# Routing logits added up by products with a matrix of ones and zeros, and fewer count products, in an attention and mixture-of-experts kernel

## Chip, cores and metric

The kernel runs on one core of a Trainium2 chip. The metric is the device time of one execution in microseconds, the median of several executions.

## What is computed

The reference runs attention with a sigmoid in place of the softmax over 8 batches of 12 heads, 448 tokens and a head size of 64. Its output, 3584 tokens of 768 numbers, goes into a layer of 8 experts, where each token is sent to the expert of its largest logit:

```
scores = scale * q @ k.T - log(S);  attn = sigmoid(scores);  x = attn @ v
logits = x @ w_gate                       # 3584 x 8
e_idx  = argmax(logits)
gate_w = softmax(logits)[e_idx]
eom    = sigmoid(x @ w_output_gate)[e_idx]
out[token] = gate_w * eom * (relu(x @ w1[e_idx]) @ w2[e_idx])
```

## The kernel before

**Attention.** TensorE works through 168 units: `scores` (L626) makes four products 64x64 by 64x448 in fp32 for two heads, ScalarE applies the sigmoid (L634), and `values` (L636) multiplies by v two units later. Seven units make a group of two head pairs; there are 24 groups, three to a batch. VectorE adds halves and transposes each finished head pair (L644 to L655), and SyncE loads the next group and stores x to DRAM.

**Gates.** After every second group, `gates(k)` (L668) multiplies four head pairs by the gate weights, both kinds of gates at once (L671). The array is cut into four column strips of 32; strip e holds head pair e's share of 16 logits for 448 tokens, and 16 rows of zeros. VectorE copies or adds these 128x448 partial sums to SBUF tile `gl` (L676 to L683).

**Routing.** `route(b)` (L229) turns a batch's `gl` into positions in the experts' lists. It is a generator, and `attention` calls its steps at fixed places of the unit loop (the named steps in L710 and L701), so the order of work on every engine is written out by hand:

- "logits": TensorE transposes `gl` in four chunks of 112 tokens (L238) into PSUM bank `mm_ps`. VectorE adds the four strips (L239), and in five short operations finds the largest logit and a 0/1 matrix `oh`, 112 tokens by 4 chunks by 8 experts, in bf16 (L242 to L246).
- "counts": TensorE counts tokens with bf16 products. A strict triangle `tri` times `oh` gives each token's rank within its chunk (L254); products of all ones add the counts of earlier chunks (L256, three products), and four more make the batch's totals `cnt` (L260).
- "places": ScalarE copies ranks and totals out of PSUM (L262); GpSimd works out positions and weights. "rows" scatters four lists of rows to DRAM.

Seven batches go through these steps inside the attention units. The last batch's run inside the first expert slot, where `side()` (L769) calls them between the `layer1` products (L467, L468).

**Start.** `constants()` (L129) issues the identity matrix, `wg`, the ones, the triangle and small tables, nearly all on GpSimd. `attention` then clears a `warm` tile on VectorE (L691), loads three groups, and issues 20 products on `warm` (L695) ahead of the first scores.

**Experts.** Each slot takes 256 tokens of one expert. Weights are split into high and low parts by ScalarE and VectorE, and TensorE does the products in fp32r (L467, L468, L490 to L492; half slots L574 to L576).

Of the kernel before, what the change touches and what calls it, by code (L numbers as in the profile page):

```python
# [9 lines left out]
F32 = mybir.dt.float32  # L10
F32R = mybir.dt.float32r
BF16 = mybir.dt.bfloat16
I32 = mybir.dt.int32
AF = mybir.ActivationFunctionType
ALU = mybir.AluOpType
AX = mybir.AxisListType
# [4 lines left out]
B, H, S, D = 8, 12, 448, 64  # L21
NPAIR = H // 2
E = 8
# [3 lines left out]
CP = 112  # L27
NCH = S // CP
# [23 lines left out]
class Kernel:  # L52
# [76 lines left out]
    def constants(self):  # L129
        nc = self.nc  # L130
        cp = self.const = self.pool("const")
        dram = self.pool("dram", space=DRAM)
        self.x_dram = dram.tile([NT * 4, Q4], F32, name="x_dram")
        self.lst = dram.tile([E * CAP + TS, 6], F32, name="lst")

        self.bias_s = cp.tile([128, 1], F32, name="bias_s")
        nc.vector.memset(self.bias_s, -math.log(S))
        nc.scalar.activation(self.warm_t(cp), self.bias_s, AF.Sigmoid)
        self.ident = cp.tile([128, 128], F32, name="ident")
        make_identity(nc, self.ident)  # L140
        self.wg = cp.tile([128, NPAIR, 32], F32, name="wg")
        nc.gpsimd.memset(self.wg, 0.0)
        nc.gpsimd.dma_start(self.wg[:, :, 0:16], self.wgo)
        self.ones = cp.tile([CP, 128], BF16, name="ones")
        nc.gpsimd.memset(self.ones, 1.0)
        self.tri = cp.tile([CP, 128], BF16, name="tri")
        nc.gpsimd.memset(self.tri, 1.0)
        nc.gpsimd.affine_select(self.tri, self.tri, pattern=[[1, 128]], compare_op=ALU.is_gt, fill=0.0,
                                base=0, channel_multiplier=-1)
        iota = lambda t, pattern, base=0: nc.gpsimd.iota(  # L150
            t, pattern=pattern, base=base, channel_multiplier=0, allow_small_or_imprecise_dtypes=True)
        self.rev = cp.tile([CP, NCH, E], F32, name="rev")
        iota(self.rev, [[0, NCH], [-1, E]], E)
        self.run = cp.tile([128, E], F32, name="run")
        nc.gpsimd.memset(self.run, 0.0)
        self.off = cp.tile([128, E], F32, name="off")
        self.ebase = cp.tile([128, E], F32, name="ebase")
        iota(self.ebase, [[CAP, E]])
        self.ids = cp.tile([1, E], F32, name="ids")
        iota(self.ids, [[1, E]])  # L160
        self.kts = cp.tile([1, 2, 16], F32, name="kts")
        iota(self.kts, [[HS, 2], [TS, 16]])
        self.meta = cp.tile([CP, B, NCH, 6], F32, name="meta")
        self.tok = cp.tile([CP, 2, NCH], I32, name="tok")
        self.tokf = cp.tile([CP, NCH, 4], F32, name="tokf")
        self.step = cp.tile([CP, B, 4], F32, name="step")
        nc.gpsimd.iota(self.tok[:, 0], pattern=[[CP, NCH]], base=0, channel_multiplier=1)
        iota(self.step, [[S, 4 * B]])
        nc.gpsimd.iota(self.meta[:, :, :, 4], pattern=[[S, B], [CP, NCH]], base=0, channel_multiplier=1,
                       allow_small_or_imprecise_dtypes=True)  # L170
        self.lt32 = [cp.tile([32, 6, 32], F32, name="lt32")]
        self.eps = cp.tile([CP, NCH], F32, name="eps")
        nc.gpsimd.memset(self.eps, 1e-9)
        self.one8 = cp.tile([1, E], F32, name="one8")
        nc.gpsimd.memset(self.one8, 1.0)
        self.last_e = cp.tile([1, 1], F32, name="last_e")
        self.taken = cp.tile([1, E], F32, name="taken")
        slots = EARLY + LATE_N
        self.lts = cp.tile([128, slots, 2, 2], I32, name="lts")
        self.ltb = cp.tile([128, E, 1, 2], I32, name="ltb")  # L180
        self.lxs = cp.tile([128, slots, 8], I32, name="lxs")
        self.lxb = cp.tile([128, E, 4], I32, name="lxb")
        self.slots = cp.tile([1, 2, LATE_N], F32, name="slots")
        for i, st in enumerate((1, TS)):
            iota(self.slots[:, i], [[st, LATE_N]])
        gl = [cp.tile([128, n], F32, name=f"gl{i}") for i, n in enumerate((2 * TS, S))]
        self.gl = [g[:, 0:S] for g in gl]
        self.sums = [gl[0][:, 0:TS], gl[0][:, TS:2 * TS], gl[1][:, 0:TS]]
        self.route_tiles()

    def row_words(self):
        v, tok = self.nc.vector, self.tok
        v.tensor_scalar(tok[:, 1], tok[:, 0], 5, None, ALU.logical_shift_right)
        v.tensor_scalar(tok[:, 0], tok[:, 0], 31, None, ALU.bitwise_and)
        v.tensor_scalar(tok[:, 0], tok[:, 0], S // 32, None, ALU.mult)
        v.tensor_tensor(tok[:, 0], tok[:, 0], tok[:, 1], ALU.add)
        v.tensor_copy(self.tokf, tok[:, 0].unsqueeze(2).broadcast_to([CP, NCH, 4]))
        for b in range(B):
            v.tensor_tensor(self.meta[:, b, :, 0:4], self.tokf,
                            self.step[:, b].unsqueeze(1).broadcast_to([CP, NCH, 4]), ALU.add)  # L200
# [11 lines left out]
    def route_tiles(self):  # L212
        rp = self.pool("route")
        t = lambda n, shape, dt=F32: rp.tile(shape, dt, name=n)
        self.R = dict(
            lg=t("lg", [CP, NCH, 16]),
            mx=t("mx", [CP, NCH]), fi=t("fi", [CP, NCH]), df=t("df", [CP, NCH, E]), rk=t("rk", [CP, NCH, E]),
            oh=t("oh", [CP, NCH, E], BF16), sg=t("sg", [CP, 3, NCH, E]),
            pc=t("pc", [128, (NCH + 1) * E]), pos=t("pos", [CP, NCH, E]), posf=t("posf", [CP, NCH]),
            t4=t("t4", [CP, NCH, 4]), t2=t("t2", [CP, NCH, 2]),  # L220
            posi=t("posi", [CP, NCH], I32), den=t("den", [CP, NCH]), eom=t("eom", [CP, NCH]))
# [7 lines left out]
    def route(self, b):  # L229
        nc, R = self.nc, self.R  # L230
        g, v = nc.gpsimd, nc.vector
        tt = g.tensor_tensor
        bc = lambda t: t.unsqueeze(2).broadcast_to([CP, NCH, E])
        tt(self.off, self.run, self.ebase, ALU.add)
        yield "logits"
        ps = self.mm_ps
        for c in range(NCH):
            nc.tensor.transpose(ps[0:CP, 128 * c:128 * c + 128], self.gl[b % 2][:, c * CP:(c + 1) * CP], self.ident)  # L238
        v.tensor_reduce(R["lg"], ps[0:CP, 0:128 * NCH].rearrange("p (c e x) -> p c x e", c=NCH, e=4)[:, :, 0:16, :],  # L239
                        AX.X, ALU.add)  # L240
        lg = R["lg"][:, :, 0:E]
        v.tensor_reduce(R["mx"], lg, AX.X, ALU.max)  # L242
        v.tensor_tensor(R["df"], lg, bc(R["mx"]), ALU.subtract)
        v.scalar_tensor_tensor(R["rk"], R["df"], 0.0, self.rev, ALU.is_ge, ALU.mult)
        v.tensor_reduce(R["fi"], R["rk"], AX.X, ALU.max)
        v.tensor_tensor(R["oh"], R["rk"], bc(R["fi"]), ALU.is_equal)  # L246
        yield "counts"
        sg, oh = R["sg"], R["oh"]
        nc.scalar.activation(sg[:, 0], R["df"], AF.Sigmoid)
        nc.scalar.activation(sg[:, 1], R["df"], AF.Sigmoid, scale=-1.0)  # L250
        nc.scalar.activation(sg[:, 2], R["lg"][:, :, E:16], AF.Sigmoid)
        ps = self.mm_ps
        pre, cnt = ps[:, 0:NCH * E], ps[:, NCH * E:(NCH + 1) * E]
        nc.tensor.matmul(pre, self.tri, oh.rearrange("p c e -> p (c e)"), start=True, stop=False)  # L254
        for c in range(NCH - 1):
            nc.tensor.matmul(pre[:, (c + 1) * E:].rearrange("p (c e) -> p c e", e=E), self.ones,  # L256
                             oh[:, c:c + 1, :].broadcast_to([CP, NCH - 1 - c, E]),
                             start=False, stop=(c == NCH - 2))
        for c in range(NCH):
            nc.tensor.matmul(cnt, self.ones, oh[:, c, :], start=(c == 0), stop=(c == NCH - 1))  # L260
        yield "places"
        nc.scalar.copy(R["pc"], ps[:, 0:(NCH + 1) * E])  # L262
        v.reciprocal(sg[:, 1], sg[:, 1])
# [487 lines left out]
    def build(self, phases="abc"):  # L751
        tc, nc = self.tc, self.nc
        ms = tc.manual_schedule()
        ms.__enter__()
        self.constants()
        self.memory()
        with tc.tile_pool(name="attn", bufs=1) as p, tc.tile_pool(name="rows", bufs=1) as q:
            rt = self.attention(p, q)
        self.late_memory()
# [110 lines left out]
```

## Time and profile before

| | |
|---|---|
| Median of 3 runs | 802.03 us (799.63, 802.03, 804.19) |
| Profiled execution, its own time | 802.2 us |
| Its span, first to last instruction | 800.4 us |
| TensorE busy (matmul) | 784.6 us, 98% |
| TensorE weight loads | 582.3 us, 73% |
| VectorE, ScalarE, GpSimd busy | 498.4, 494.9 and 338.4 us |
| Mean granted TensorE clock | 0.996 |

The span is what the trace covers; the time is some 2 us longer. PE stands for matrix products and PEld for the weight loads that run beside them. A product's row begins when it can be issued and includes its way through the array, so rows overlap: how much a group of products holds TensorE up is read from start to start, not from durations. Attention lasts to about 285 us, the experts from there to the end.

### The profile page before, as it was taken

How to read it: one execution, taken by the hardware profiler on the slowest of the kernel's cores; microseconds unless marked ns; L12 is line 12 of the kernel's file. 1: busy time of each engine (PE TensorE's matmuls, PEld its weight loads, DVE VectorE, ACT ScalarE, POOL GpSimd, SP SyncE). 2: the span in 40 equal slices, each digit the busy share in tenths (PEclk: the TensorE clock that was granted, in tenths of full speed). 3: DMA queues.
4: the chain of work that ended last, by engine and by line, in shares of the span. 5: the costliest groups of instructions: out<-in, count | busy, mean ns of one | idle time of the engine just before them, and what ended most of it. 6: DMA issues, size and time to landing. Idle time of an engine off the chain costs nothing. (4 is left out here: it accounts for less than half of the span.)

```text
span 800.4 us, 15091 instructions
## 1 busy us (share of the span) xinstructions
PE 784.6 (98%) x5772; PEld 582.3 (73%) x5772; DVE 498.4 (62%) x731; ACT 494.9 (62%) x665; POOL 338.4 (42%) x454
## 2 busy tenths in 40 slices
PE   9999999999999899899999999999999999999996
PEld 4333433333333379799999999999999999999885
DVE  2344435444455667877785657766667767667687
ACT  5666666666668556556665556655666557565685
POOL 4003302310333456647646265543646725445344
PEclk9999999999999999999999999999999999999999
DMA  6353553525448420237228471182274211749382
GB/s 255 131 209 128 158 200 139 193 85 208 170 173 347 154 90 21 77 123 266 75 75 290 166 270 51 49 312 79 61 259 156 64 45 41 267 131 336 110 314 59
DMA packets 32311, 126.80 MB, mean 158 GB/s; under 512 B 5536, under 2 KB 7824, under 8 KB 28257
## 3 DMA queue, kind: packets, MB, share of 16 engines
q1 hardware_dynamic: 22288, 100.81, 35.5%
q0 software_dynamic: 9936, 24.88, 9.4%
q8 instruction: 50, 0.82, 0.4%
q14 instruction: 37, 0.29, 0.1%
HBM read 153.15 MB, written 23.64 MB: 221 GB/s over the span
## 5 line engine op out<-in xcount | busy, mean ns | idle before, releaser
L467 PE MATMUL ps<-rounded 128*128 128x512 f32 x672 | 234.8, 393 | 2.0 <-DVE gl L476 2.0
L634 ACT ACTIVATE a<-ps,bias_s 128x896 f32<-128x896 f32 x168 | 169.2, 1008 | 102.5 <-PE ps L632 96.1
L468 PE MATMUL ps<-rounded 128*128 128x256 f32 x672 | 188.1, 280 | 0.0
L404 POOL DMA_INDIRECT plain<-x_dram,lxs x120 | 170.2, 1418 | 38.3 <-issue 37.0
L490 PE MATMUL ps<-w2h,h 128*128 128x384 f32 x480 | 160.6, 335 | 0.0
L492 PE MATMUL ps<-w2h,h 128*128 128x384 f32 x480 | 160.4, 334 | 0.0
L491 PE MATMUL ps<-w2l,h 128*128 128x384 f32 x480 | 160.4, 334 | 0.0
L632 PE MATMUL ps<-kqv 64*64 64x448 f32 x1344 | 158.6, 543 | 0.5 <-ACT a L634 0.4
L641 PE MATMUL ps<-a,kqv 64*64 64x448 f32 x1344 | 156.7, 538 | 0.0
L427 DVE TENSOR_TENSOR w2l<-plain,w2h 128x1536 fp32r<-128x1536 f32 x60 | 105.3, 1758 | 78.3 <-ACT w2h L426 68.1
L467 PEld LDWEIGHTS ps<-rounded 128*128 128x128 f32 x672 | 125.7, 187 | 31.3 <-DVE gl L476 2.7
L504 POOL DMA_INDIRECT out<-y,lts x28 | 59.7, 2132 | 172.3 <-ACT y L502 92.5
L468 PEld LDWEIGHTS ps<-rounded 128*128 128x128 f32 x672 | 127.0, 189 | 0.0
L641 PEld LDWEIGHTS ps<-a,kqv 64*64 64x64 f32 x1344 | 51.7, 134 | 75.5 <-issue 74.8
L632 PEld LDWEIGHTS ps<-kqv 64*64 64x64 f32 x1344 | 48.8, 133 | 75.1 <-issue 62.3
L433 DVE TENSOR_TENSOR rounded<-plain,rounded 128x2048 fp32r<-128x2048 f32 x46 | 102.8, 2284 | 0.0
L426 ACT CAST w2h<-plain 128x1536 fp32r<-128x1536 f32 x60 | 88.2, 1473 | 5.4 <-PE ps L671 4.4
L490 PEld LDWEIGHTS ps<-w2h,h 128*128 128x128 f32 x480 | 90.1, 188 | 0.7
L491 PEld LDWEIGHTS ps<-w2l,h 128*128 128x128 f32 x480 | 90.1, 188 | 0.1
L492 PEld LDWEIGHTS ps<-w2h,h 128*128 128x128 f32 x480 | 90.1, 188 | 0.0
L475 ACT COPY gl<-ps 128x256 f32<-128x256 f32 x112 | 41.7, 372 | 77.7 <-PE ps L468 73.3
L430 ACT CAST rounded<-plain 128x2048 fp32r<-128x2048 f32 x46 | 87.6, 1904 | 0.0
(186 smaller groups left out, 649.0 us busy)
## 6 DMA issues: line engine op xcount, KB each, us to landing
plain<-w SPq DMA_DIRECT2D x68, 768.0 KB
plain<-w SPq DMA_DIRECT2D x48, 1024.0 KB
kqv<-kqv SPq DMA_DIRECT2D x23, 1344.0 KB
x_dram<-xt SPq DMA_DIRECT2D x8, 1344.0 KB
plain<-w SPq DMA_DIRECT2D x6, 512.0 KB
plain<-x_dram,lxs POOLq DMA_INDIRECT x120
kqv<-kqv SPq DMA_DIRECT2D x1, 896.0 KB
lst<-plain POOLq DMA_DIRECT2D x1, 726.0 KB
```

Source lines behind the costliest of these rows:

```text
L404: self.nc.gpsimd.indirect_dma_start(out=s["xg"][:, g], out_offset=None, in_=x4, in_offset=bass.IndirectOffsetOnAxis(ap=s["lx"][:, g:g + 1] ...
L426: self.nc.scalar.copy(hi, raw)
L427: self.nc.vector.tensor_tensor(lo, raw, r32(hi), ALU.subtract)
L433: self.nc.vector.tensor_tensor(self.w1p[1][k], self.w1r[:, 2 * k:2 * k + 2], r32(self.w1p[0][k]), ALU.subtract)
L467: nc.tensor.matmul(ps, wh[d][:, c], self.xc[:, d].rearrange("p a t -> p (a t)"), start=(d == 0), stop=False)
L468: nc.tensor.matmul(ps[:, 0:TS], wl[d][:, c], self.xc[:, d, 0], start=False, stop=(d == 5))
L490: nc.tensor.matmul(ps, hh[:, f, tk], wh, start=(f == 0), stop=False)
L491: nc.tensor.matmul(ps, hh[:, f, tk], wl, start=False, stop=False)
L492: nc.tensor.matmul(ps, hl[:, f, tk], wh, start=False, stop=(f == 7))
L632: nc.tensor.matmul(ps[half[h], j, 0:S], kg[half[j], e, 0, o:o + 64], kg[half[j], e, 1], start=True, stop=True)
L634: nc.scalar.activation(at[u % 4], ps[:, :, 0:S], AF.Sigmoid, bias=self.bias_s, scale=1.0 / math.sqrt(D))
L641: nc.tensor.matmul(self.ps_o[e][h][half[j], 0:S], v[half[h], 6 if i == 3 else 3 * e + c, j], a[half[h], j], start=(i in ((0, 3 if h else 4 ...
```

## The change

The transposes of "logits" become four fp32 products of the same `gl` chunks with `pick`, a 128x16 matrix whose column x has ones in rows x, x+32, x+64 and x+96. They give the 16 sums themselves, 112 tokens by 16, and VectorE copies them out. `pick` is made at the start by a VectorE reduction of the identity matrix, ahead of the clearing of `warm` in VectorE's order. In "counts", `oh` gets a fifth chunk of zeros, cleared once on GpSimd; the totals become the fifth chunk of the ranks, so that one triangle product and four products of ones remain. Two small tables, `tokf` and `step`, move into the big tile `plain`, and `memory()` is called ahead of `constants()`.

```diff
@@ constants
         make_identity(nc, self.ident)
+        self.pick = cp.tile([128, 16], F32, name="pick")
+        nc.vector.tensor_reduce(self.pick, self.ident.rearrange("p (e x) -> p x e", e=4)[:, 0:16], AX.X, ALU.add)
...
-        self.tokf = cp.tile([CP, NCH, 4], F32, name="tokf")
-        self.step = cp.tile([CP, B, 4], F32, name="step")
+        self.tokf = self.carve(0, NCH, 4, dt=F32, parts=CP)
+        self.step = self.carve(256, B, 4, dt=F32, parts=CP)
...
         self.route_tiles()
+        nc.gpsimd.memset(self.R["oh"][:, NCH], 0.0)
@@ route_tiles
-            oh=t("oh", [CP, NCH, E], BF16), sg=t("sg", [CP, 3, NCH, E]),
+            oh=t("oh", [CP, NCH + 1, E], BF16), sg=t("sg", [CP, 3, NCH, E]),
@@ route
         for c in range(NCH):
-            nc.tensor.transpose(ps[0:CP, 128 * c:128 * c + 128], self.gl[b % 2][:, c * CP:(c + 1) * CP], self.ident)
-        v.tensor_reduce(R["lg"], ps[0:CP, 0:128 * NCH].rearrange("p (c e x) -> p c x e", c=NCH, e=4)[:, :, 0:16, :],
-                        AX.X, ALU.add)
+            nc.tensor.matmul(ps[0:CP, 16 * c:16 * c + 16], self.gl[b % 2][:, c * CP:(c + 1) * CP], self.pick,
+                             start=True, stop=True)
+        v.tensor_copy(R["lg"], ps[0:CP, 0:16 * NCH].rearrange("p (c x) -> p c x", c=NCH))
...
-        v.tensor_tensor(R["oh"], R["rk"], bc(R["fi"]), ALU.is_equal)
+        oh = R["oh"][:, 0:NCH]
+        v.tensor_tensor(oh, R["rk"], bc(R["fi"]), ALU.is_equal)
...
-        pre, cnt = ps[:, 0:NCH * E], ps[:, NCH * E:(NCH + 1) * E]
-        nc.tensor.matmul(pre, self.tri, oh.rearrange("p c e -> p (c e)"), start=True, stop=False)
-        for c in range(NCH - 1):
-            nc.tensor.matmul(pre[:, (c + 1) * E:].rearrange("p (c e) -> p c e", e=E), self.ones,
-                             oh[:, c:c + 1, :].broadcast_to([CP, NCH - 1 - c, E]),
-                             start=False, stop=(c == NCH - 2))
+        pre = ps[:, 0:(NCH + 1) * E].rearrange("p (c e) -> p c e", e=E)
+        nc.tensor.matmul(pre, self.tri, R["oh"], start=True, stop=False)
         for c in range(NCH):
-            nc.tensor.matmul(cnt, self.ones, oh[:, c, :], start=(c == 0), stop=(c == NCH - 1))
+            nc.tensor.matmul(pre[:, c + 1:], self.ones, oh[:, c:c + 1, :].broadcast_to([CP, NCH - c, E]),
+                             start=False, stop=(c == NCH - 1))
@@ build
-        self.constants()
         self.memory()
+        self.constants()
```

On VectorE at the start of the program, before:

```order
L137 MEMSET bias_s 128x1
L691 MEMSET rounded 128x256
L644 COPY xh<-ps 128x448
L654 TENSOR_TENSOR x_158<-xh,ps 128x448
L655 STREAM_TRANSPOSE xt_163<-x_158 128x14x32
```

and with the change (line numbers are one or more higher there):

```order
L137 MEMSET bias_s 128x1
L142 TENSOR_REDUCE pick<-ident 128x16
L692 MEMSET rounded 128x256
L645 COPY xh<-ps 128x448
L655 TENSOR_TENSOR x_159<-xh,ps 128x448
L656 STREAM_TRANSPOSE xt_164<-x_159 128x14x32
```

The reduction, which needs GpSimd's identity matrix, now stands ahead of the clearing of `warm` (a part of `rounded`), for which the first 20 products wait.

On TensorE, the "counts" step of the first batch between two attention units, before:

```order
L641 MATMUL ps<-a_155,kqv_152 64x448 x4
L254 LDWEIGHTS tri
L254 MATMUL ps<-oh,tri 128x32
L256 LDWEIGHTS ones
L256 MATMUL ps<-oh,ones 128x24
L256 MATMUL ps<-oh,ones 128x16
L256 MATMUL ps<-oh,ones 128x8
L260 LDWEIGHTS ones
L260 MATMUL ps<-oh,ones 128x8
```

(each product of ones has a load ahead of it, shown once for each line, and the last product, L260, stands there four times) and with the change:

```order
L642 MATMUL ps<-a_156,kqv_153 64x448 x4
L258 LDWEIGHTS tri
L258 MATMUL ps<-oh,tri 128x40
L260 LDWEIGHTS ones
L260 MATMUL ps<-oh,ones 128x32
L260 MATMUL ps<-oh,ones 128x24
L260 MATMUL ps<-oh,ones 128x16
L260 MATMUL ps<-oh,ones 128x8
```

Eight pairs of load and product have become five; what stands around them is the same. The "logits" step keeps its place and its four rows, which read `ps<-pick,gl 112x16` in place of `ps<-ident,gl 112x128`.

## Rows read from the trace of the kernel before

**Rows 1.** The page's first two parts: busy time of each engine over the span, and TensorE's busy tenths in 40 slices.

```profile
PE 784.6 (98%) x5772; PEld 582.3 (73%) x5772; DVE 498.4 (62%) x731; ACT 494.9 (62%) x665; POOL 338.4 (42%) x454
...
PE   9999999999999899899999999999999999999996
```

**Rows 2.** What TensorE waited for over the whole span: total us, times, longest us.

```profile
PE ps L671 <- DVE x L654: 2.1, 1, 2.1
PE ps L467 <- DVE gl L476: 2.0, 2, 1.5
PE ps L695 <- DVE rounded L691: 1.3, 1, 1.3
PE ps L574 <- DVEq L823: 1.2, 1, 1.2
PE ps L671 <- issue: 0.6, 2, 0.5
PE ps L632 <- ACT a L634: 0.4, 1, 0.4
```

**Rows 3.** TensorE in order of time around the "logits" and "counts" steps of the first batch (start us, duration us, engine, line, operation, count).

```profile
57.30 0.93 PE L641 MATMUL ps<-a,kqv 64*64 64x448 f32 x8
58.16 0.65 PE L238 MATMUL ps<-ident,gl 128*112 128x128 f32 x4
58.74 0.98 PE L632 MATMUL ps<-kqv 64*64 64x448 f32 x8
...
60.30 0.93 PE L632 MATMUL ps<-kqv 64*64 64x448 f32 x8
61.05 0.93 PE L641 MATMUL ps<-a,kqv 64*64 64x448 f32 x8
61.91 0.19 PE L254 MATMUL ps<-oh,tri 112*128 112x32 bf16 x1
...
62.20 0.98 PE L632 MATMUL ps<-kqv 64*64 64x448 f32 x8
```

**Rows 4.** The groups of instructions by line, products and weight loads: count, busy us, mean ns of one (then idle time before them).

```profile
L632 PE MATMUL ps<-kqv 64*64 64x448 f32 x1344 | 158.6, 543 | 0.5 <-ACT a L634 0.4
L671 PE MATMUL ps<-x,wg 128*32 128x448 f32 x96 | 12.9, 555 | 2.8 <-DVE x L654 2.1 <-issue 0.6
L238 PE MATMUL ps<-ident,gl 128*112 128x128 f32 x32 | 5.1, 283 | 0.0
...
L671 PEld LDWEIGHTS ps<-x,wg 128*32 128x32 f32 x96 | 2.1, 108 | 11.2 <-issue 8.2 <-DVE x L654 2.7 <-DVE xt L655 0.3
L632 PEld LDWEIGHTS ps<-kqv 64*64 64x64 f32 x1344 | 48.8, 133 | 75.1 <-issue 62.3 <-ACT a L634 12.5
L467 PEld LDWEIGHTS ps<-rounded 128*128 128x128 f32 x672 | 125.7, 187 | 31.3 <-DVE gl L476 2.7 <-issue 1.4
L238 PEld LDWEIGHTS ps<-ident,gl 128*112 128x112 f32 x32 | 3.3, 133 | 5.0 <-DVE xh L644 4.9
L260 PEld LDWEIGHTS <-ones 112*128 112x128 bf16 x32 | 1.4, 95 | 0.0
```

**Rows 5.** Weight loads in order of time around the last batch's "logits" step, in the first expert slot.

```profile
290.07 0.47 PEld L238 LDWEIGHTS ps<-ident,gl 128*112 128x112 f32 x4
290.51 0.19 PEld L467 LDWEIGHTS ps<-rounded 128*128 128x128 f32 x1
290.62 0.19 PEld L468 LDWEIGHTS ps<-rounded 128*128 128x128 f32 x1
```

**Rows 6.** Products in order of time there, and around that batch's "counts" step.

```profile
290.06 0.28 PE L468 MATMUL ps<-rounded 128*128 128x256 f32 x1
290.18 0.60 PE L238 MATMUL ps<-ident,gl 128*112 128x128 f32 x4
290.54 0.48 PE L467 MATMUL ps<-rounded 128*128 128x512 f32 x1
290.85 0.28 PE L468 MATMUL ps<-rounded 128*128 128x256 f32 x1
290.97 0.40 PE L467 MATMUL ps<-rounded 128*128 128x512 f32 x1
...
296.97 0.19 PE L254 MATMUL ps<-oh,tri 112*128 112x32 bf16 x1
297.01 0.22 PE L256 MATMUL ps<-oh,ones 112*128 112x24 bf16 x3
297.09 0.24 PE L260 MATMUL ps<-oh,ones 112*128 112x8 bf16 x4
297.27 0.50 PE L467 MATMUL ps<-rounded 128*128 128x512 f32 x1
```

**Rows 7.** A narrow window of the first batch's "logits" step: the first transpose, and the second and third loads.

```profile
58.16 0.32 PE L238 MATMUL ps<-ident,gl 128*112 128x128 f32 x1
...
58.21 0.24 PEld L238 LDWEIGHTS ps<-ident,gl 128*112 128x112 f32 x2
```

**Rows 8.** GpSimd, VectorE and TensorE in order of time at the start.

```profile
1.10 0.29 POOL masks.py:199 TENSOR_SCALAR_AFFINE_SELECT ident<-ident 128x128 f32<-128x128 f32 x1
...
4.20 0.15 POOL L150 IOTA step<- 112x32 f32 x1
...
0.98 0.27 DVE L691 MEMSET rounded<- 128x256 f32 x1
...
1.31 4.45 PE L695 MATMUL ps<-rounded 128*128 128x256 f32 x20 [1.31 <-DVE rounded L691]
5.68 1.74 PE L632 MATMUL ps<-kqv 64*64 64x448 f32 x16
```

**Rows 9.** VectorE's work on the logits in the first batch: the attention's transposition ahead of it, the sum, the largest logit, and `oh`.

```profile
58.94 0.65 DVE L655 STREAM_TRANSPOSE xt<-x 128x448 f32<-128x448 f32 x1
59.51 0.38 DVE L239 TENSOR_REDUCE lg<-ps 112x64 f32<-112x256 f32 x1
59.92 0.18 DVE L242 TENSOR_REDUCE mx<-lg 112x4 f32<-112x32 f32 x1
...
60.82 0.19 DVE L246 TENSOR_TENSOR oh<-rk,fi 112x32 bf16<-112x32 f32 x1
```

**Rows 10.** VectorE's wait for a list from DRAM late in attention, and the stretch after it by stage (us, then busy us and count of each engine, granted clock, DMA share, GB/s).

```profile
260.96 0.50 DVE L388 STREAM_TRANSPOSE lt<-plain 32x192 f32<-32x192 f32 x1 [4.21 <-DMA plain<-lst]
...
264.80:268.20 3.40, 3.40 (x17) 1.04 (x20) 1.24 (x2) 2.05 (x3) 1.51 (x10) 0.50 1.04 403
```

More of the change, by code (lines that the diff above doesn't have):

```diff
@@ L245, in route @@
         v.tensor_reduce(R["fi"], R["rk"], AX.X, ALU.max)
-        v.tensor_tensor(R["oh"], R["rk"], bc(R["fi"]), ALU.is_equal)
+        oh = R["oh"][:, 0:NCH]
+        v.tensor_tensor(oh, R["rk"], bc(R["fi"]), ALU.is_equal)
         yield "counts"
-        sg, oh = R["sg"], R["oh"]
+        sg = R["sg"]
         nc.scalar.activation(sg[:, 0], R["df"], AF.Sigmoid)
@@ L754, in build @@
         ms.__enter__()
+        self.memory()
         self.constants()
-        self.memory()
         with tc.tile_pool(name="attn", bufs=1) as p, tc.tile_pool(name="rows", bufs=1) as q:
```

## Prediction

> **What bounds the kernel.** I read the page's busy shares first, then what TensorE waited for, then the stretches in which the changed steps lie. TensorE is busy 98% of the span, in nearly every slice of both stages [rows 1], and all its waits come to 7.6 us [rows 2]; the reader is to see that no other engine leaves a gap worth hiding work in. Around the changed steps that holds exactly: scores and values follow each other every 0.75 us, no wait between them, except where a routing step is put in [rows 3]. So whatever such a step takes from TensorE, start to start, is added to the time, and work on VectorE counts only if it makes TensorE wait. The sum below is TensorE's time at three places: "logits", "counts" and the start.
>
> **What a "logits" step costs now.** In attention the values at 57.30 would be followed by scores at 58.05, and are at 58.74; the transposes with the change of array shape before and after take 0.69 us. From the first transpose to the next scores it is 0.58 us [rows 3]: a first load of about 0.05, four transposes 0.108 apart (four loads begin in the 0.44 us from 290.07 to 290.51 [rows 5]), and 0.10 until the array has changed shape again. In the expert slot, four transposes hold the next product back by 0.36 us, from 290.18 to 290.54, and that product is 0.08 longer than its like, because its load was not covered [rows 6]: 0.44 us.
>
> **What it will cost.** Both versions load the same `gl` chunks as weights, 112 columns; only what streams past them shrinks, from 128 columns to 16. If the streaming set the pace, this would be a gain. But two things in the trace speak against it. First, an fp32 product is two pairs of load and product, a transpose is one: L632 issues 168 x 4 = 672 products and has 1344 records, L671 48 products and 96 records, L238 32 transposes and 32 records [rows 4]. So four products make eight loads. Second, loads take time by their columns: 108 ns for 32, 133 for 64, 187 for 128 [rows 4]. That is some 80 ns of way, which loads share, and 0.83 ns a column; where two loads of 128 columns follow one another with nothing else between them, they begin 0.11 us apart [rows 5], which fits. 112 columns then take 0.093 to 0.096 us. The streaming is small: a unit's scores are eight records of 448 columns, four at a time in the four corners of the array, and take 0.75 us [rows 3], so a record of 16 columns takes 0.375 x 16/448 = 0.013 us, and disappears beside a load. I take 0.096 us for each of eight records.
>
> - Attention: 8 x 0.096 + 0.013 + 0.10 = 0.88 us against 0.58, **+0.30** for each of seven batches, +2.1.
> - Expert slot: the first load is covered by the product before it, as at 290.07 [rows 5, 6]; 7 x 0.096 and then 0.11 for the next product's uncovered load make 0.78 against 0.44, **+0.34**.
>
> Together **+2.4 us**. No row shows an fp32 load of 112 columns for a real product, so it needs bounds. Below: loads as quick as those of the bf16 count products, which follow 0.025 to 0.027 apart [rows 6]. Then attention is 8 x 0.025 + 0.11 = 0.31, that is -0.27 each, and the slot 7 x 0.025 + 0.11 = 0.285, or -0.15: -2.0 together. Above: a load that begins only when the one before has ended, 80 + 93 = 173 ns: 8 x 0.173 + 0.11 = 1.49, that is +0.91, and 7 x 0.173 + 0.11 - 0.44 = +0.88 in the slot: +7.3. I take the middle because fp32 loads of three widths lie on one line, and the bf16 load, 95 ns for 128 columns, is plainly of another kind.
>
> **"Counts".** Eight products become five. In the slot the three L256 products take 0.08 us from 297.01 to 297.09 [rows 6], so 0.027 each, whatever their 8 to 24 columns; eight more columns in the triangle product and its followers cost at most a few ns. Three fewer save 0.08 us in each batch, **-0.6 us** in all.
>
> **Start.** `pick` puts a wait into VectorE's queue: the identity matrix is ready at 1.39 us, while `warm` was cleared from 0.98 [rows 8]. Behind the reduction stands that clearing, and behind that the 20 first products. The reduction reads 64 numbers a partition; L242 reads 32 in 0.18 us and L239 256 in 0.38 [rows 9], so 0.21. Clearing then begins near 1.69 instead of 0.98, and the products near 2.0 instead of 1.31: **0.7 us later**. Nothing covers it, since the scores at 5.68 follow the 20 products directly, with no DMA wait between [rows 8]. But those products run at the lower of TensorE's clock levels (20 in 4.45 us, 0.22 us apart, where L468's like ones take 0.12 [rows 6, 8]). If the clock rises at the same moment as before, near the end of the 20, the last three or four of them now run at 2.4 GHz instead of 1.2 and give back 0.4. So 0.3 to 0.7; no row says which, and I take **+0.5**. The nearest row, the pace up to the first scores, allows either.
>
> **What costs nothing.** VectorE's copy of 64 numbers should take about 0.2 in place of 0.38, 1.4 us in eight batches, but `oh` is ready at 61.01 and TensorE comes to the counts at 61.8 [rows 3, 9]; in the other direction, the transposes end at 58.81 [rows 3] and L239 begins at 59.51, behind L655 [rows 9], so logits that arrive 0.3 later still wait for VectorE, not it for them. The fifth chunk's clearing on GpSimd at the start is needed at the first counts, 61.91 [rows 3]. `tokf` and `step` in `plain` add a wait for GpSimd to the first load of expert weights, which comes late in attention, and `step` was written at 4.20 [rows 8]. The largest of TensorE's waits, 2.1 us near 262, hangs on a list from DRAM [rows 2, 10] whose load is issued when the units reach it; no changed step lies between that and the wait, so it moves along and hides nothing.
>
> **Sum.** +2.4 - 0.6 + 0.5 = **+2.3 us**. The sum is made against the profiled execution's 802.2 us; the median of the runs, 802.03, is 0.2 below it. So I predict **804.3 us**, +0.3%. Less than 0.5%, 4.0 us, is about what a measurement of this kernel can tell from no change: its three runs alone spread over 4.6 us.
>
> **The rivals.**
>
> *The loads are quick and the change gains.* With the lower bound the sum is -2.0 - 0.6 + 0.5 = -2.1, **799.9 us**. For it: the transposes load the same fp32 `gl` in 133 ns, about 54 beyond the way, not 93 [rows 4]; if real products keep that rate, eight loads of 0.056 take 0.45 and the step costs what it did, so the time would be 802.0. Against: fp32 loads of products on the line above. The Trainium skill, TensorEngine Tiling, "Instruction Overhead", gives each matmul about 60 cycles and says that one with a single column takes as long as one with 60; by that alone a 16-column product costs 25 ns (an estimate from that page) and this rival would be right. The 0.025 us between count products agree with it, but those have bf16 weights, and no run here shows it for fp32.
>
> *The loads don't overlap, and it gets slower.* If each of the eight loads waits until the one before has gone its whole way, the sum is +7.3 - 0.6 + 0.5 = +7.2, **809.2 us**; more than +0.5% begins where a record takes 0.117 us instead of 0.096. Against: the second transpose's load begins at 58.21, 0.05 us into a first product that lasts 0.32 [rows 7]. The Trainium skill, TensorE: Matmul & The Clock Gate, "The mechanism" under row/col tiling, says that a load overlaps products in flight only when its row group differs; here all loads use all 128 rows, so by that sentence this rival holds. The trace disagrees, as the 58.21 row stands for the same rows of the array.
>
> *The clock rises later, or falls once more.* After TensorE's wait near 262 the granted clock was 0.50 for 3.4 us [rows 10], 1.7 us of lost work. If the later start costs another such stretch, the time is 804.3 + 1.7 = **806.0 us**. For it: the first products are at 1.2 GHz and start later. Against: the changed steps open no gap in which TensorE is idle.
>
> *It does not show at all.* If the waits shrink by what the steps grow, it stays at **802.0 us**. Against: the argument on the list above, and most of the other waits lie behind the changed steps.
>
> **How the numbers follow.** Forecast 60%, quick loads 20%, no overlap 8%, the clock 7%, no effect 5%. With a median of few runs moving by 1 to 2 us, the forecast falls above 806.0 in about one case in six; with all of the no-overlap case and half of the clock's that is 21% slower. Under 798.0 needs the quick loads and a lucky median: 5%. The remaining 74% lie within 0.5%. The range of 8 in 10 runs from the quick loads' 799.9, rounded down to 800.0, up to 807.5, the clock's case with its spread; it leaves the case without overlap out.
>
> **What would show it.** In the changed profile: 64 product records on the `pick` line instead of 32, loads of about 173 ns that begin 0.093 to 0.097 apart, and 0.88 us from the first to the next scores; five count products, 0.03 us or so apart; first product near 2.0 us and first scores between 6.0 and 6.4; VectorE's copy near 0.2 us with no wait of TensorE for `oh`. The prediction is wrong if loads begin 0.06 apart or less, or 0.12 or more, if the first scores still begin near 5.7, or if a new TensorE wait stands at the counts.

## The result: 0.5% slower

| | before | changed |
|---|---|---|
| Median of 19 runs | 799.63 us | 803.89 us |
| Lowest, highest | 798.37, 804.19 | 802.72, 807.04 |
| Ratio of the changed to the kernel before, 95% interval | | 1.0051 (1.0042 to 1.0061) |
| Profiled execution, its span | 802.2, 800.4 us | 803.49, 801.8 us |

The time lies 0.4 us from the forecast, but the step from before is +4.3 us and not +2.3: the three runs known ahead of the prediction had a median 2.4 us above that of 19. So 2 us are still to be found.

The busy shares of the changed kernel [rows 1], and the group of 512-column products of the experts' first layer, first before, then with the change:

```profile
L467 PE MATMUL ps<-rounded 128*128 128x512 f32 x672 | 234.8, 393 | 2.0 <-DVE gl L476 2.0
```

```profile
PE 788.1 (98%) x5780; PEld 585.0 (73%) x5780; DVE 497.4 (62%) x732; ACT 495.2 (62%) x665; POOL 322.0 (40%) x455
...
L468 PE MATMUL ps<-rounded 128*128 128x512 f32 x672 | 238.7, 399 | 2.4 <-DVE gl L477 2.4
```

TensorE has 8 records more (32 for the logits, 24 fewer for the counts) and 3.5 us more work. The 6 ns between the means, 393 and 399, are a surprise: no instruction of the first layer was changed.

What TensorE waited for (us, times, longest) [rows 2]:

```profile
PE ps L468 <- DVE gl L477: 2.4, 2, 1.9
PE ps L696 <- DVE rounded L692: 2.0, 1, 2.0
PE ps L575 <- PEq L824: 1.3, 1, 1.3
PE ps L672 <- DVE x L655: 0.6, 1, 0.6
PE ps L633 <- ACT a L635: 0.4, 1, 0.4
```

No wait at the counts. At the start it is 2.0 us for 1.3. The longest wait for VectorE's `gl`, in the second expert slot, is 1.9 us where it was 1.5. The wait for VectorE's x near 262 us is 0.6 where the first profile of before had 2.1.

TensorE in order of time around the first batch's two steps [rows 3]:

```profile
57.84 0.93 PE L642 MATMUL ps<-a,kqv 64*64 64x448 f32 x8
58.70 0.96 PE L241 MATMUL ps<-pick,gl 128*112 128x16 f32 x8
59.59 0.98 PE L633 MATMUL ps<-kqv 64*64 64x448 f32 x8
...
61.90 0.93 PE L642 MATMUL ps<-a,kqv 64*64 64x448 f32 x8
62.76 0.19 PE L258 MATMUL ps<-oh,tri 112*128 112x40 bf16 x1
62.80 0.24 PE L260 MATMUL ps<-oh,ones 112*128 112x32 bf16 x4
62.97 0.98 PE L633 MATMUL ps<-kqv 64*64 64x448 f32 x8
```

"Logits" goes from 58.70 to 59.59, 0.89 us where the transposes took 0.58; "counts" from 62.76 to 62.97, 0.21 where it was 0.29, 61.91 to 62.20 [rows 3].

The weight loads of that step, in two narrow windows:

```profile
58.70 0.27 PEld L241 LDWEIGHTS ps<-pick,gl 128*112 128x112 f32 x2 [0.70 <-DVE xh L645]
...
58.80 0.37 PEld L241 LDWEIGHTS ps<-pick,gl 128*112 128x112 f32 x3
```

One load lasts 0.17 to 0.18 us. Loads 2 to 4 begin at 58.80 and the last of them ends at 59.17, so they begin 0.10 apart, each while the one before is still under way.

The start [rows 8], and VectorE's part of the logits [rows 9]:

```profile
1.42 0.26 DVE L142 TENSOR_REDUCE pick<-ident 128x16 f32<-128x64 f32 x1 [0.47 <-POOL ident masks.py:199]
1.69 0.27 DVE L692 MEMSET rounded<- 128x256 f32 x1
...
2.01 4.28 PE L696 MATMUL ps<-rounded 128*128 128x256 f32 x20 [2.01 <-DVE rounded L692]
6.22 1.74 PE L633 MATMUL ps<-kqv 64*64 64x448 f32 x16
...
60.05 0.18 DVE L243 COPY lg<-ps 112x64 f32<-112x64 f32 x1
...
61.16 0.19 DVE L250 TENSOR_TENSOR oh<-rk,fi 112x32 bf16<-112x32 f32 x1
```

First product at 2.01, first scores at 6.22, 0.54 later than before. The copy takes 0.18 us; `oh` is ready at 61.35, 1.4 us ahead of its use.

### The profile page after: what moved, and what is told of

Its sections match the earlier page's. It is cut to its first block, busy times and chain, and to the rows that moved or that the text cites. A ratio compares the mean times of both kernels' runs of the same rounds, so it can differ in the third digit from the quotient of the medians.

```text
span 801.8 us, 15110 instructions
## 1 busy us (share of the span) xinstructions
PE 788.1 (98%) x5780; PEld 585.0 (73%) x5780; DVE 497.4 (62%) x732; ACT 495.2 (62%) x665; POOL 322.0 (40%) x455
## 5 line engine op out<-in xcount | busy, mean ns | idle before, releaser
L468 PE MATMUL ps<-rounded 128*128 128x512 f32 x672 | 238.7, 399 | 2.4 <-DVE gl L477 2.4
L405 POOL DMA_INDIRECT plain<-x_dram,lxs x120 | 162.0, 1350 | 38.3 <-issue 34.8
L505 POOL DMA_INDIRECT out<-y,lts x28 | 52.2, 1864 | 191.3 <-ACT y L503 118.0
```

The costliest lines, as they stand in the source:

```text
L405: self.nc.gpsimd.indirect_dma_start(out=s["xg"][:, g], out_offset=None, in_=x4, in_offset=bass.IndirectOffsetOnAxis(ap=s["lx"][:, g:g + 1] ...
L468: nc.tensor.matmul(ps, wh[d][:, c], self.xc[:, d].rearrange("p a t -> p (a t)"), start=(d == 0), stop=False)
```

## The experiments

Ratios and differences are to the kernel before as it was timed beside each experiment: 799.21 us for e1 to e4, 804.69 for e5 to e8, 799.53 for e9 to e11, 801.84 for e12. Slot lengths are those of slots in which TensorE waits for nothing.

The two traces gave a suspect. In the changed kernel the expert slots from the third on are 33.60 us apart, from first product to first product; before, 33.28. All 0.32 us arise in the first layer, 40 ns in each of its eight steps of six product pairs. The pairs of the changed kernel (512 and 256 columns, in order of time in a slot without waits):

```profile
491.40 0.40 PE L468 MATMUL ps<-rounded 128*128 128x512 f32 x1
491.63 0.28 PE L469 MATMUL ps<-rounded 128*128 128x256 f32 x1
491.75 0.40 PE L468 MATMUL ps<-rounded 128*128 128x512 f32 x1
...
492.46 0.40 PE L468 MATMUL ps<-rounded 128*128 128x512 f32 x1
```

and of the kernel before (a second profile, e10_before_again):

```profile
455.58 0.39 PE L467 MATMUL ps<-rounded 128*128 128x512 f32 x1
455.81 0.28 PE L468 MATMUL ps<-rounded 128*128 128x256 f32 x1
455.92 0.39 PE L467 MATMUL ps<-rounded 128*128 128x512 f32 x1
...
456.62 0.39 PE L467 MATMUL ps<-rounded 128*128 128x512 f32 x1
```

Three pairs take 1.06 us in the one and 1.04 in the other, through whole slots. Since the instructions are the same, the places of tiles in memory were the first theory, and the routing itself its rival.

**e1_place.** Only the order of two calls:

```diff
-        self.constants()
         self.memory()
+        self.constants()
```

> The kernel before with memory() called ahead of constants() and nothing else: the big tile rounded begins at byte 16512 of a partition instead of 27584. Theory P (place): the first-layer products of the experts read rounded, and its place alone makes each expert slot 33.6 us instead of 33.28 from first product to first product; time about 4 us above the kernel before (+0.5%). Theory R (routing): the slots are longer because of the routing's new products and VectorE work; then the slots stay at 33.28 us and the time within 0.5 us of the kernel before.

Measured: 799.02 us, ratio 1.0006 (0.9987 to 1.0024); slots 33.30 us; mean of the 512-column product:

```profile
L467 PE MATMUL ps<-rounded 128*128 128x512 f32 x672 | 235.3, 394 | 2.0 <-DVE gl L476 2.0
```

The place of `rounded`, from which the slowed products read everything, costs 0.02 us a slot. Theory P in this form falls.

**e2_routing_old_place.** The changed kernel with the old order of the calls:

```diff
-        self.memory()
         self.constants()
+        self.memory()
+        self.tokf = self.carve(0, NCH, 4, dt=F32, parts=CP)
+        self.step = self.carve(256, B, 4, dt=F32, parts=CP)
...
+        self.pad = cp.tile([128, 24], F32, name="pad")
```

> The whole change of the routing (products with pick, five count products, the reduction at the start), but constants() ahead of memory() as before, with 96 unused bytes so that rounded begins at 27584 again, and the table step written after the other constants. Theory P: slots 33.28 us, the steps in attention cost as in the changed kernel (8 loads 0.098 us apart, first scores 0.5 us later), time 2.4 us above the kernel before (+0.3%). Theory R: slots 33.6 us, time as of the changed kernel, about 4.3 us above.

Measured: 801.88 us, 1.0034 (1.0021 to 1.0047), that is +2.7 us; slots 33.28, attention's steps as in the changed kernel. Theory R falls too: with the same instructions on TensorE the slots are as before. The routing alone costs +2.7 us (1.7 to 3.8) where +2.3 was forecast.

**e3_after_64** and **e4_before_minus64.** The changed kernel with `rounded` moved by 64 bytes, and the kernel before with `rounded` moved down by 64:

```diff
+        self.pad = self.pool("pad").tile([128, 16], F32, name="pad")     # e3, ahead of rounded
...
-        self.last_e = cp.tile([1, 1], F32, name="last_e")                # e4: both to a pool behind plain
-        self.taken = cp.tile([1, E], F32, name="taken")
```

> The changed kernel with 64 unused bytes ahead of rounded, which then begins at 16576, an odd multiple of 64 as 27584 is, instead of 16512, a multiple of 128. If the slots' 0.32 us hang on the place within 128 bytes: slots 33.28 us and some 4 us less than the changed kernel, so near or 0.5 us below the kernel before plus 2.4 less what the rest gave back, about 0 to +0.1%. If they hang on the place at large (which part of the memory): slots 33.6 us and the time of the changed kernel, +0.5%.

> The kernel before with two small tiles (64 bytes) moved behind plain, so that rounded begins at 27520, a multiple of 128, instead of 27584; nothing else changes. If the place within 128 bytes decides: slots 33.6 us and about 4 us above the kernel before (+0.5%). If the place at large decides: slots 33.28 us and no change.

Measured: e3 804.52 us, 1.0073 (1.0053 to 1.0092), slots 33.60; e4 799.24, 0.9997 (0.9983 to 1.001), slots 33.30. The place within 128 bytes does not decide. Both answers fit "the place at large", but e1 had `rounded` exactly where the changed kernel has it. What the changed kernel and e3 share, and the fast ones don't, lies elsewhere: their late tiles (attention's, then h, w2h, w2l and y in the same place) begin at byte 150368 and 150432 of a partition, odd multiples of 32, and in before, e1, e2 and e4 at 150464.

**e5_after_late96** and **e6_before_late32.** Only those tiles are moved, each way:

```diff
         self.memory()
         self.constants()
+        self.gap = self.pool("gap").tile([128, 24], F32, name="gap")     # e5, in the changed kernel
...
         self.constants()
         self.memory()
+        self.gap = self.pool("gap").tile([128, 8], F32, name="gap")      # e6, in the kernel before
```

> The changed kernel with 96 unused bytes between the small tables and the tiles that come and go (attention's, later h, w2h, w2l, y), which then begin at 150464 as before instead of 150368, an odd multiple of 32; rounded stays at 16512. Theory L (late tiles): where those tiles begin sets how layer 2 hands over to layer 1, and with it which of two rhythms layer 1 falls into: slots fall back from 33.60 to 33.30 us, pairs of first-layer products from 353 to 347 ns, and the time from 4.3 to about 2.5 us above the kernel before (+0.3%). Theory R (the routing itself, or the order of instructions, sets the rhythm): slots stay at 33.60 us and the time at +0.5 to +0.7%.

> The kernel before with 32 unused bytes behind plain, so that the late tiles begin at 150496, an odd multiple of 32; rounded stays at 27584 and no instruction changes. Theory L: slots 33.60 us instead of 33.28, pairs 353 ns, time 2 to 4 us above the kernel before (+0.25 to +0.5%). Theory R: slots 33.28 us and no change.

The 512-column products of e5, then of e6:

```profile
L468 PE MATMUL ps<-rounded 128*128 128x512 f32 x672 | 235.4, 393 | 2.7 <-DVE gl L477 2.7
```

```profile
L467 PE MATMUL ps<-rounded 128*128 128x512 f32 x672 | 238.5, 399 | 1.9 <-DVE gl L476 1.9
```

Slots 33.30 and 33.59 us where they were 33.60 and 33.28: 96 bytes take the slow rhythm out of the changed kernel, 32 bytes put it into the kernel before. In time e6 is 1.0029 (1.0011 to 1.0046), +2.3 us, as expected; e5 is 1.0053 (1.0033 to 1.0072), which was not: its slots were fast and its time was not.

Its waits show where some of that went, in that execution:

```profile
PE ps L468 <- DVE gl L477: 2.7, 3, 1.9
PE ps L672 <- issue: 2.0, 6, 0.8
...
PE ps L493 <- DVE h L482: 1.3, 1, 1.3
```

**e12_after_late96_again.** The kernel of e5 again.

> The kernel of e5_after_late96 again, whose first timing (+0.53%, 0.33 to 0.72) was no better than the changed kernel's +0.51% although its first layers ran in the fast rhythm. Its trace had 5 us near 262 us and 1.6 us near 379 us in which TensorE waited for issue or VectorE, which other kernels had in some executions. If those belong to executions: about 2.6 us above the kernel before here (+0.33%), as e2_routing_old_place, slots 33.30 us, no such waits. If the places of the late tiles bring them: +0.5% again, with the same waits.

Measured: 804.82 us beside 801.84, 1.0041 (1.0018 to 1.0065), +3.3 us; slots 33.30. The 1.3 us wait for `h`, at 379 us in e5, is gone, and e7 and e8 below have it, so it belongs to executions. Waits for issue (time in which TensorE waited for nothing that the profile shows) were there again near 262 us:

```profile
PE ps L672 <- issue: 1.4, 4, 0.9
```

This does not settle whether e5's version is faster than the changed kernel: the interval holds both +2.6 and +4.1. Nor does it rule out that these places bring the waits near 262 us: of the four profiles with the changed order and a gap (e5, e8, e9, e12) only e9 is without them.

**e7_counts_only** and **e11_counts_again.** The kernel before with five count products; `step` moves and 96 unused bytes are added, so that `rounded` and the late tiles stay in place:

```diff
-        pre, cnt = ps[:, 0:NCH * E], ps[:, NCH * E:(NCH + 1) * E]
...
+        pre = ps[:, 0:(NCH + 1) * E].rearrange("p (c e) -> p c e", e=E)
+        nc.tensor.matmul(pre, self.tri, R["oh"], start=True, stop=False)
+        self.step = self.carve(256, B, 4, dt=F32, parts=CP)              # room for the fifth chunk
```

> The kernel before with the five count products alone: transposes and VectorE's sum stay, there is no matrix of ones and zeros and no wait at the start, rounded and the late tiles begin where they did. By the prediction's step: 0.077 us less in each batch, 0.6 us less in all (-0.08%), slots 33.28 us, first scores near 5.6 us; a time that cannot be told from the kernel before, but 0.077 in each batch's steps in the trace. Rival: the fewer products only make TensorE wait elsewhere, and the batch takes what it took.

> The kernel of e7_counts_only again, beside a profile of the kernel before on the same chip. By the trace its steps are 0.6 us shorter, yet it was timed 0.18% slower (0 to 0.35%). If that was the spread of waits that hang on transfers and not on the five products: a ratio within 0.2% of 1 here, the same 0.077 us in each batch, and waits near 262, 325 and 380 us that both kernels show. If the five products really cost time: slower by 0.2% again, and a longer wait or step that the kernel before doesn't have.

The first batch's counts in e7:

```profile
61.76 0.19 PE L255 MATMUL ps<-oh,tri 112*128 112x40 bf16 x1
61.79 0.24 PE L257 MATMUL ps<-oh,ones 112*128 112x32 bf16 x4
61.97 0.98 PE L630 MATMUL ps<-kqv 64*64 64x448 f32 x8
```

and in the kernel before (e10_before_again):

```profile
61.79 0.19 PE L254 MATMUL ps<-oh,tri 112*128 112x32 bf16 x1
61.83 0.22 PE L256 MATMUL ps<-oh,ones 112*128 112x24 bf16 x3
61.90 0.24 PE L260 MATMUL ps<-oh,ones 112*128 112x8 bf16 x4
62.07 0.98 PE L632 MATMUL ps<-kqv 64*64 64x448 f32 x8
```

0.21 against 0.28, in each of the six batches between the groups at 15 and 254 us: 238.18 us from the one to the other against 238.62. The time doesn't show it: 1.0018 (1.0000 to 1.0035), then 1.0010 (0.9997 to 1.0022). A gain of 0.6 us is under what the waits move, and this version does not beat the kernel before.

**e8_pick32.** `pick` with 32 columns, so twice the streaming past the same loads:

```diff
-        self.pick = cp.tile([128, 16], F32, name="pick")
+        self.pick = cp.tile([128, 32], F32, name="pick")
...
-            nc.tensor.matmul(ps[0:CP, 16 * c:16 * c + 16], self.gl[b % 2][:, c * CP:(c + 1) * CP], self.pick,
+            nc.tensor.matmul(ps[0:CP, 32 * c:32 * c + 32], self.gl[b % 2][:, c * CP:(c + 1) * CP], self.pick,
```

> The changed kernel with a matrix of 32 columns instead of 16, so that each of the four products streams twice the columns past the same weights (16 zero sums are not read); late tiles at 150464. If the weight loads set the pace: loads begin 0.098 us apart as with 16 columns, and the step takes 0.89 us from its first load to the next scores, at most 0.02 more. If the streaming or a fixed cost for each product set it: 0.11 or more apart, 1.0 us.

```profile
59.34 0.97 PE L241 MATMUL ps<-pick,gl 128*112 128x32 f32 x8
60.24 0.61 PE L633 MATMUL ps<-kqv 64*64 64x448 f32 x4
```

0.90 us against 0.89. Eight records that stream twice the columns take 0.01 more in all: the streamed columns do not set the pace.

**e9_clear_first.** e5 with `warm` cleared ahead of the reduction:

```diff
+        nc.vector.memset(r32(self.rounded[:, 0:256]), 0.0)
         self.pick = cp.tile([128, 16], F32, name="pick")
...
-        nc.vector.memset(r32(warm), 0.0)
```

> The changed kernel with late tiles at 150464 as in e5_after_late96, and the clearing of warm ahead of the reduction that makes pick, in VectorE's order. If the wait for the identity matrix is what delays the start: first product at 1.31 us instead of 2.01, first scores between 5.5 and 5.9 as the clock rises, and everything behind them earlier by as much as the first scores. If something else in the change delayed the first scores, they stay later than 6.0 us with the first product at 1.31.

```profile
1.30 4.64 PE L696 MATMUL ps<-rounded 128*128 128x256 f32 x20 [1.30 <-DVE rounded L141]
5.87 2.18 PE L634 MATMUL ps<-kqv 64*64 64x448 f32 x16
8.43 0.98 PE L634 MATMUL ps<-kqv 64*64 64x448 f32 x8 [0.39 <-ACT a L636]
```

The first product is back at 1.30 and the first scores came at 5.87, inside the range, so the wait for the identity matrix did hold up the start. But the gain was lost in this execution: all 20 products ran at the pace of the lower clock level, 0.23 us apart (4.57 us from 1.30 to 5.87), and so did the first of the scores (the 16 score records take 2.18 us where they took 1.74 [rows 8]), and the second group of units began at 16.00 us, later than in the changed kernel's profile (15.90). Its one time, 800.99, says nothing.

**e10_before_again.** The kernel before, second profile.

> The kernel before once more, for a second profile beside the others of this call. If the 5 us by which its first profile was behind the others near 262 us belong to that execution alone, the stretch from the first scores of the group at 254 us to those of the next takes 13.0 us here and not 18.2. If they belong to the kernel, 18 us again. In both cases the slots take 33.28 us.

The stretch took 13.1 us, so the 5 us near 262 us in the first profile belonged to that execution. Two of its slots took 33.69 and 34.35 us, with waits for the low parts of weights; the others 33.28. This profile is the one to compare stages with.

**The stages, side by side** (us, from the starts of products in the traces: first scores; from the scores of the second group to those of the group at 254 us; from inside the third slot to the start of the last full slot, ten first layers; and the same from the start of the third slot):

```
                          first    attention   ten first from third
                          scores   groups      layers    slot on
before, first profile      5.68    238.62      341.12     366.08
before, e10                5.56    238.62      342.61     367.57
changed                    6.22    240.03      344.32     369.60
e1_place                   5.58    238.62      342.77     367.75
e2_routing_old_place       6.58    240.02      341.95     366.91
e3_after_64                6.58    240.02      344.32     369.60
e4_before_minus64          5.63    238.62      344.25     369.23
e5_after_late96            5.88    240.03      341.32     368.70
e6_before_late32           5.80    238.62      344.25     369.53
e7_counts_only             5.53    238.18      341.12     369.89
e8_pick32                  6.69    240.11      341.32     370.05
e9_clear_first             5.87    240.02      342.02     367.00
e11_counts_again           5.48    238.18      343.76     368.72
e12_after_late96_again     6.40    240.03      341.32     366.93
```

The attention column is the same to 0.01 us in every kernel with the same routing, whatever the places. The ten first layers take 344.25 to 344.32 in the three slow-rhythm kernels, and 341.1 to 344.3 in the eleven profiles with the fast one, 342.14 in the mean. So the slow rhythm costs 3.2 us there if nothing else waits, and 2.2 on average: the faster first layers run into waits for the low parts of the weights, in e11 this one between 390 and 745 us, where the changed kernel and e6 have none. That column begins behind the third slot's waits, which only profiles with the fast rhythm have (the slot is 2.4 to 3.8 us longer in e5, e7 and e8). Counted with them, in the last column, it is 369.5 to 369.6 against 368.08 in the mean, and the slow rhythm costs 1.5.

```profile
PE ps L466 <- DVE rounded L431: 1.4, 2, 1.0
```

## Why the prediction was right, and what it missed

**The bound.** TensorE's time, start to start, was added to the time in attention, as forecast: the attention column moves by six times a batch's difference and by nothing else.

**"Logits".** Forecast +0.30 a batch in attention; measured 0.31 (0.89 against 0.58). Eight records, loads of 0.17 to 0.18 us, 0.10 apart where 0.093 to 0.097 had been given. The line through fp32 loads of 32, 64 and 128 columns [rows 4] held for 112, and e8 shows that the streamed columns are not what is paid. That it is the loads' columns, and not a fixed cost of each fp32 record, rests on that line alone: no run changed the loads. For the last batch the two steps together added 0.18 us between the first slot's first and second layer (18.96 us in e10, 19.14 changed), 0.26 by the forecast.

**"Counts".** Forecast -0.08 a batch; measured 0.21 against 0.28 in e7, -0.07 to -0.08.

**Start.** Forecast +0.5, between 0.3 and 0.7; +0.54 against the first profile, +0.66 against the second. The reduction took 0.26, not 0.21, and the first product came at 2.01. But this term was given too narrow, and on average too small: when the clock rises is not fixed to the start. In e2, e3 and e8 the first scores came at 6.58 to 6.69, up to 1.1 us later than the kernel before's, and e9's second group began 0.8 us later than e10's though its first product came early. In the six profiles with the first product near 2.0 us the second group of units begins at 15.56 to 16.79 us, 16.20 in the mean; in the seven without the reduction at 15.16 to 15.48, 15.29 in the mean. That is 0.9 us and not 0.5. The rival of a clock that rises later is thus real, as a spread from execution to execution.

**What costs nothing.** VectorE's copy, GpSimd's clearing and the wait of the first weight load behaved as forecast. The wait for the list near 262 us stayed where it was, 0.6 to 0.7 us in the undisturbed profiles. One wait that grew has no term in the prediction: in the second slot TensorE waits for `gl` behind VectorE's work on the table of slots, 1.4 to 1.5 us at the longest in six of the seven profiles with the old transposes and 1.8 to 2.2 in all seven with `pick`. Why VectorE gets to it some 0.4 us later was not followed up.

**The sum.** At the scores that follow the seventh batch's counts the changed kernel is 2.2 us behind e10:

```profile
268.84 0.98 PE L632 MATMUL ps<-kqv 64*64 64x448 f32 x8
...
271.02 0.98 PE L633 MATMUL ps<-kqv 64*64 64x448 f32 x8
```

With the 0.2 of the first slot that is +2.4 for +2.3. With the longer wait in the second slot it is 2.7 us behind at the third slot's first product (354.88 for 352.20). e2, which has the routing alone, has +2.7 us (1.7 to 3.8). In the prediction, +0.5% would begin where a record takes 0.123 us and not 0.117 (63 records, 1.7 us above the sum); nothing hangs on it.

**The miss.** The step "what costs nothing" spoke of `tokf` and `step` only as a wait, and of the order of memory() and constants() not at all. The order alone leaves the late tiles where they were, at 150464 in e1. But `tokf` and `step` take 192 bytes out of each partition ahead of them, and `pick` and the fifth chunk put 96 back, so they begin 96 bytes lower, at 150368. e5 and e6 show that moving these tiles alone switches the first layers' rhythm: 0.32 us a slot, 1.5 to 2.2 us in all after the waits it replaces. With +2.7 that is +4.2 to +4.9, where +4.3 (3.4 to 4.9) was measured. So the forecast of the change was short by this term; that the time itself was met is luck: the first three runs of before, from which it was counted, lay 2.4 us high. Of the rivals, quick loads and loads without overlap are out: 0.10 us apart is neither 0.03 nor 0.17.

**What stays open.** Why 32 bytes in tiles that the first layer doesn't read change its pace. Only one place with the fast rhythm was tried, 150464, and three with the slow one, so it isn't shown either that odd multiples of 32 are the rule. What the traces show is that the rhythm is entered, not fixed: in e10, with the fast places, it changes in the middle of a slot after a wait.

```profile
486.08 0.39 PE L467 MATMUL ps<-rounded 128*128 128x512 f32 x1
...
487.12 0.39 PE L467 MATMUL ps<-rounded 128*128 128x512 f32 x1
488.03 0.39 PE L468 MATMUL ps<-rounded 128*128 128x256 f32 x1 [0.52 <-DVE rounded L433]
...
488.96 0.40 PE L467 MATMUL ps<-rounded 128*128 128x512 f32 x1
...
490.02 0.40 PE L467 MATMUL ps<-rounded 128*128 128x512 f32 x1
```

Three pairs take 1.04 us ahead of the wait (486.08 to 487.12) and 1.06 behind it (488.96 to 490.02), with the same instructions; the next slot is fast again. In e6, with slow places, the second slot ends at the fast pace behind its waits, three pairs in 1.04 us:

```profile
335.29 0.39 PE L467 MATMUL ps<-rounded 128*128 128x512 f32 x1
...
336.33 0.39 PE L467 MATMUL ps<-rounded 128*128 128x512 f32 x1
```

From the third slot on, all 36 first layers of the three slow-rhythm profiles are slow, and 5 of the 132 of the others, four of them behind such a wait. That the second layer, which does read the late tiles, hands over to the first at another moment is a guess that fits; it was not tested. Nor was its rival, that ScalarE and VectorE write the late tiles (h, w2h and w2l) while the first layer runs; the change of pace in e10 and e6 at fixed places speaks against a cause that lies in the places alone. Times did not separate e5's version from the changed kernel.

## What to carry to other kernels

A small fp32 product in place of a transpose has two weight loads where the transpose has one; here shrinking the streamed side gained nothing, 0.01 us for half the columns. When an edit adds or moves tiles, compare the pace of stages it does not touch: a third to a half of this change's cost came from where other tiles ended up, and only moving the tiles alone (unused bytes, no other edit) told it apart. Put nothing ahead of the first instruction that the busiest engine waits for.

## What was not expected of the hardware

- First-layer products on unchanged operands have two stable rhythms, 1.04 and 1.06 us for three pairs of 512 and 256 columns. From the third slot on, the three kernels whose late tiles began at 150368, 150432 and 150496 ran in the slower one in each slot; the others, at 150464, in the faster one but for one slot each in e1, e4, e5, e9 and e10.
- Near 262 us, in some executions of several kernels (the first profile of before, e5, e7, e8, e12), TensorE's products came 0.7 us apart or more though they waited for nothing that the profile names. The stretch from the group at 254 us to the next took 17.2 to 19.2 us there, and 13.0 to 13.3 in eight of the other nine profiles (14.7 in e6). The DMA engines were nearly always busy, but no less so in e10 (a share of 0.88 to 1.02 from 258 to 266 us), which has no such waits, so this does not tell the executions apart and the cause stays open. How much of the spread between runs it makes is not shown: the two profiled executions of the kernel before differ by 5.1 us in this stretch and by 1.2 in their times.
